# Attention scores in units of two key chunks by 512 queries instead of one chunk by 576, with the last 64 queries of a head in a unit of their own

## The chip, the cores and the metric

One core of a Trainium2 chip runs the whole program. The metric is device time in microseconds (us) from the start to the end of one execution, and the number given for the kernel before is the median of three runs. The engines are named as the profile names them: PE (TensorE matmul), PEld (its weight loads), DVE (VectorE), ACT (ScalarE), POOL (GpSimd) and SP (SyncE, which here only issues DMAs).

## The reference

Attention over 8 batches, 8 heads, 1152 keys and 576 pooled queries of width 64, followed by a mixture of experts that picks one expert of eight for each token.

```python
def _attn_ref(q, k, v):                       # q, k, v: (8, 8, 1152, 64)
    q_pool = q.reshape(B, H, S // 2, 2, D).mean(axis=3)
    scores = scale * np.matmul(q_pool, k.transpose(0, 1, 3, 2))
    scores = scores - np.max(scores, axis=-1, keepdims=True)
    attn = np.exp(scores)
    attn = attn / (np.sum(attn, axis=-1, keepdims=True) + 1e-09)
    return np.matmul(attn, v)

def _moe_ref(x, w_gate, w_output_gate, w1, w2):   # x: (4608, 512), 8 experts
    e_idx = np.argmax(x @ w_gate, axis=1)         # then for each expert e and its tokens:
    h = np.maximum(x[mask] @ w1[e], 0.0)
    out[mask] = gate_w[mask, None] * eom[mask, e, None] * (h @ w2[e])
```

## The kernel before

The attention stage works on 32 pairs of heads, four pairs to a batch. The experts' stage follows it. All numbers that need more than 16 bits are split in a high and a low float16 part, and products are summed from the parts.

For every pair there are four streams of work, and the order of the instructions on PE, DVE, ACT and POOL is the order in which the program writes them (`manual_schedule`):

- **Maxima** (`mgen`): the largest score of each query, found ahead of time. For a tile of 128 queries and a third of the keys (384) one matmul goes to one of three PSUM banks (`mp`, L320), and DVE reduces it to one column (`pm`, L321). A pair has 9 tiles of queries, so 27 such steps. They run one pair ahead. A small float32 transpose (L355), a DVE split (`mr`, L360) and a DMA bring the maxima into row 64 of `qb`, from where they enter the scores as one more term of the product.
- **Scores** (`scores`): one step is one chunk of 128 keys by all 576 queries of a head, so 18 steps for a pair. Four matmuls of 288 columns (L383 and L384, twice) fill two banks of one of two PSUM slots, `SP[0]` and `SP[1]`, taken in turn. ACT then takes the exponential twice: once as float16, `ph`, and once as float32. In odd steps (`PLP`) the float32 one stays in the slot (L402, L403), and DVE subtracts `ph` from it, bank by bank (`pl`, L407); the slot is free after that. In even steps the float32 one goes to SBUF (`p32`, L412, L413), the slot is free after the second exponential, and POOL subtracts (L414).
- **P V** (`av`): for each chunk and each of five blocks of 128 queries (the last one overlaps the fourth by 64) three matmuls of 65, 64 and 65 columns (L429 to L431), 270 for a pair, into one bank. They run `ALAG` = 6 steps behind the scores, in bursts (`BURST`) of two chunks in every other step. DVE normalises the result of a head (`norm`, L439 to L441).
- **Preparation and routing**: loads, scalings and splits of the next pairs' q, k and v (`prep`: ACT L237, L249, L277; POOL L240 to L252, L281, L284; DMAs by SP), transposes and router products of finished pairs (`logits`, L481 to L493), and after each fourth pair the routing of a batch (`router`), with five indirect DMAs on POOL (L593).

The main loop goes through 18 steps for a pair; in a step come, in this order, what waits in `pendv` (the DVE subtraction of the step before), the routers, the scores, one or two steps of maxima, and the P V burst. `tc.declare_no_dep` lets the matmuls of a slot's first bank start when DVE has finished that bank alone.

## Time and profile before

| | |
|---|---|
| median of three runs | 1332.72 us (1332.58 to 1333.58) |
| profiled execution | 1328.25 us, its span 1326.2 us |
| attention stage | ends at about 883 us of the span; the experts' stage takes the rest |
| mean granted TensorE clock | 0.992 of full speed |

The rows of the trace are in the section on rows. Starts and durations are in us from the start of the span. A matmul's duration contains the time that it takes to pass through the engine, so the time it occupies is the distance from its start to the next start; neighbouring instructions on ACT and DVE overlap at their ends as well.

### The profile page before, as it was taken

What the parts mean: (1) busy time and instruction counts of PE and PEld (TensorE: products, weight loads), DVE (VectorE), ACT (ScalarE), POOL (GpSimd) and SP (SyncE); (2) the same over time, 40 slices, a digit from 0 to 9 for tenths busy, and PEclk for the clock granted to TensorE, in tenths of its full rate; (3) what the DMA queues carried; (4) which work ended last, traced back from release to release, by engine and by line L of the source; (5) the groups of instructions that cost most, each with busy time, mean ns of one, the idle gap of its engine ahead of it and who ended that gap; (6) DMA issues with size and microseconds to landing.
All of it is one profiled execution on the core that took longest, in us unless ns stands there. A gap on an engine that the chain in (4) does not pass through costs nothing. (4 is left out here: it accounts for less than half of the span.)

```text
span 1326.2 us, 39965 instructions
## 1 busy us (share of the span) xinstructions
PE 1259.5 (95%) x15664; PEld 939.4 (71%) x15664; DVE 1088.3 (82%) x2595; ACT 1055.0 (80%) x1944; POOL 887.0 (67%) x763
## 2 busy tenths in 40 slices
PE   6999999999999999999999899998999999999997
PEld 3777777777767777777777776775667676767775
DVE  8888888888888888888888788778786767677887
ACT  6999889989989989989989788875565656566785
POOL 5888798888888889789879798756233233333431
PEclk9999999999999999999999899999999999999999
DMA  5456364445445445345535544349967676767850
GB/s 170 130 143 173 107 149 121 142 119 136 123 132 146 117 113 171 115 117 145 148 105 153 160 139 111 83 156 322 400 232 269 227 264 228 253 241 254 287 187 16
DMA packets 101272, 225.57 MB, mean 170 GB/s; under 512 B 17980, under 2 KB 33552, under 8 KB 101075
## 3 DMA queue, kind: packets, MB, share of 16 engines
q1 hardware_dynamic: 91170, 201.41, 49.9%
q0 software_dynamic: 9056, 20.85, 4.5%
q8 instruction: 125, 2.05, 0.6%
q10 hardware_dynamic: 848, 0.66, 0.2%
q14 instruction: 73, 0.59, 0.1%
HBM read 160.04 MB, written 22.50 MB: 138 GB/s over the span
## 5 line engine op out<-in xcount | busy, mean ns | idle before, releaser
L321 DVE TENSOR_REDUCE pm<-mp 128x1 f32<-128x384 f32 x864 | 449.4, 549 | 47.2 <-PE mp L320 41.6
L414 POOL TENSOR_TENSOR pl<-p,ph 128x576 f16<-128x576 f32 x291 | 375.4, 1293 | 117.3 <-ACT ph L413 98.3
L383 PE MATMUL sps<-qa,ka 128*128 128x288 f16 x1152 | 314.6, 285 | 16.2 <-DVE pl L407 9.0
L384 PE MATMUL sps<-qb,kb 65*128 65x288 f16 x1152 | 317.0, 288 | 3.3 <-DMA qb<-mr 3.3
L429 PE MATMUL av<-vt,ph 128*128 128x65 f16 x2880 | 292.9, 193 | 1.5 <-DVE xb L441 1.0
L431 PE MATMUL av<-vt,pl 128*128 128x65 f16 x2880 | 292.6, 192 | 1.4 <-POOL pl L414 1.4
L430 PE MATMUL av<-vt,ph 128*128 128x64 f16 x2880 | 293.0, 194 | 0.0
L429 PEld LDWEIGHTS <-ph 128*128 128x128 f16 x2880 | 265.9, 97 | 24.2 <-DVE xb L441 10.4
L407 DVE TENSOR_TENSOR pl<-sps,ph 128x288 f16<-128x288 f32 x558 | 228.5, 451 | 58.7 <-ACT sps L403 54.1
L430 PEld LDWEIGHTS <-ph 128*128 128x128 f16 x2880 | 264.7, 97 | 14.0 <-issue 0.3
L431 PEld LDWEIGHTS <-pl 128*128 128x128 f16 x2880 | 265.2, 99 | 1.5 <-POOL pl L414 1.5
L402 ACT ACTIVATE ph<-sps 128x576 f16<-128x576 f32 x279 | 187.2, 671 | 64.3 <-PE sps L384 55.4
L320 PE MATMUL mp<-ka,qa 128*128 128x384 f16 x768 | 215.8, 328 | 12.9 <-DVE pm L321 9.8
L965 PE MATMUL hps<-x,w1h 128*128 128x256 f16 (+2 forms) x1408 | 206.9, 260 | 1.7 <-DVE x L953 1.7
L412 ACT ACTIVATE p<-sps 128x576 f32<-128x576 f32 x291 | 193.5, 665 | 15.1 <-PE sps L384 13.7
L413 ACT ACTIVATE ph<-sps 128x576 f16<-128x576 f32 x291 | 194.0, 667 | 0.0
L403 ACT ACTIVATE sps<-sps 128x576 f32<-128x576 f32 x279 | 186.7, 669 | 0.0
L965 PE MATMUL hps<-x,w1l 128*128 128x256 f16 (+2 forms) x704 | 178.5, 260 | 0.0
L384 PEld LDWEIGHTS <-kb 65*128 65x128 f16 x1152 | 111.7, 97 | 76.1 <-issue 21.9
L979 ACT ACTIVATE hh<-hps 128x512 f16<-128x512 f32 (+2 forms) x88 | 48.2, 549 | 119.1 <-PE hps L965 116.8
L965 PEld LDWEIGHTS <-w1h 128*128 128x128 f16 x1408 | 131.7, 98 | 15.4
L383 PEld LDWEIGHTS <-ka 128*128 128x128 f16 x1152 | 117.7, 102 | 34.9 <-issue 8.7
(284 smaller groups left out, 2304.9 us busy)
## 6 DMA issues: line engine op xcount, KB each, us to landing
vp<-in_vL_dram SPq DMA_DIRECT2D x32, 576.0 KB
qp<-in_qT_dram SPq DMA_DIRECT2D x31, 576.0 KB
kpf<-in_kT_dram SPq DMA_DIRECT2D x31, 576.0 KB
ka<-xk SPq DMA_DIRECT2D x120, 144.0 KB
raw1a<-in_w_dram SPq DMA_DIRECT2D x16, 1024.0 KB
raw2a<-in_w_dram SPq DMA_DIRECT2D x16, 1024.0 KB
raw1b<-in_w_dram SPq DMA_DIRECT2D x14, 1024.0 KB
raw2b<-in_w_dram SPq DMA_DIRECT2D x14, 1024.0 KB
```

Source lines behind the costliest of these rows:

```text
L320: nc.tensor.matmul(mp, lhsT=l, rhs=r, start=j == 0, stop=j == len(ops) - 1)
L321: nc.vector.tensor_reduce(out=pm[:, i:i + 1], in_=mp, axis=AX.X, op=ALU.max)
L383: mm = [nc.tensor.matmul(sps[:, j, 0:288], lhsT=ka[:, h, ks], rhs=qa[:, o + 288 * j:o + 288 * j + 288], start=True, stop=False), nc.tensor ...
L384: nc.tensor.matmul(sps[:, j, 0:288], lhsT=kb[:, h, ks], rhs=qb[:, h, 288 * j:288 * j + 288], start=False, stop=True)]
L407: l = nc.vector.tensor_tensor(out=pl[:, 288 * j:288 * j + 288], in0=x[:, j], in1=ph2[:, j], op=ALU.subtract)
L412: nc.scalar.activation(out=p32.rearrange("p (j n) -> p j n", j=2), in_=x, func=AF.Exp, scale=1.0 / 16 / KS)
L413: e_ = nc.scalar.activation(out=ph2, in_=x, func=AF.Exp, scale=1.0 / 16 / KS)
L414: nc.gpsimd.tensor_tensor(out=pl, in0=p32, in1=ph, op=ALU.subtract)
L429: nc.tensor.matmul(av_[:, qb, 0:65], lhsT=hi, rhs=vt[:, h, c, 0:65], start=c == 0 and qb == 0, stop=False)
L430: nc.tensor.matmul(av_[:, qb, 0:64], lhsT=hi, rhs=vt[:, h, c, 66:130], start=False, stop=False)
L431: mm = nc.tensor.matmul(av_[:, qb, 0:65], lhsT=lo, rhs=vt[:, h, c, 0:65], start=False, stop=c == NC - 1 and qb == 4)
L965: d['mm'] = nc.tensor.matmul(hp[:, f, 0:w], lhsT=W1[l][g][:, c, fs], rhs=d['x'][:, c, o:o + w], start=c == 0 and i == 0, stop=c == 3 and i ...
```

## The change

A pair now has 11 units in place of 18 steps, listed in `UNITS`. Nine units 'D' are two key chunks by the first 512 queries of a head (18 chunks of the pair in order, so that the fifth one holds the last chunk of the first head and the first chunk of the second). Two units 'T' are the last 64 queries of a head with all nine chunks. The two PSUM slots are still taken in turn; since 11 is odd, a unit's slot changes from pair to pair. Units 0, 2, 4, 6, 8, 10 (`GPS`) go to POOL, the other five, all of type D, to DVE.

- Maxima: pieces of 512 keys, two for each tile; the remaining 128 keys of up to four tiles share a bank and one reduction. 21 steps for a pair in place of 27, two in a unit (one in the first T).
- P V: pieces of one chunk by four blocks, 12 matmuls; a T unit gives 27 matmuls. They run `ULAG` = 3 units behind the scores, and the pieces stand between the steps of maxima. In the units in which a head is finished (`CLOSE`) all pieces come first and the normalisation follows at once.
- Buffers: five pairs of `ph`/`pl` for D, two for T, three `p32` of 1024 columns, where there were nine, and six of 576.
- The DMA of the maxima is issued two steps later (`SLAG`), a pair's router work one step later (`DL`). The last block of 64 queries sits in partitions 0 to 63, so one of five transposes is half as large, and two copies to `xT` take the place of three.

```diff
-BURST = {0: 2, 2: 2, 4: 2, 6: 2, 8: 1, 10: 2, 12: 2, 14: 2, 16: 3}
-PLP = (1, 3, 5, 7, 9, 11, 13, 15, 17)
+UNITS = (('D', 0), ('D', 1), ('D', 2), ('D', 3), ('T', 0), ('D', 4), ('D', 5), ('D', 6), ('D', 7), ('D', 8), ('T', 1))
+PV = (((0, 2),), ((2, 4),), ((4, 6),), ((6, 8),), (0,), ((8, 9),), ((9, 12),), ((12, 14),), ((14, 16),), ((16, 18),), (1,))
+GPS = (0, 2, 4, 6, 8, 10)
+CLOSE = (5, 10)
+ULAG = 3
+SLAG = 2
+AHEAD = 21
+MX = (2, 2, 2, 2, 1, 2, 2, 2, 2, 2, 2)
-ALAG = 6
-PB = 9
-P32 = 6
+PB = 5
+PT = 2
+P32 = 3
...
-                    ch = [(t, c) for t in range(t0, t1) for c in range(3)]
+                    ch = [((t,), c) for t in range(t0, t1) for c in range(2)]
+                    ch += [(tuple(range(t, min(t + 4, t1))), 2) for t in range(t0, t1, 4)]
...
-                        nc.vector.tensor_reduce(out=pm[:, i:i + 1], in_=mp, axis=AX.X, op=ALU.max)
+                        o = pm3[:, ts[0] - t0:ts[-1] + 1 - t0, c]
+                        nc.vector.tensor_reduce(out=o, in_=mp[:, 0:w * len(ts)].rearrange("p (t k) -> p t k", t=len(ts)), axis=AX.X, op=ALU.max)
...
+            if kind == 'D':
+                ph = pp.tile([128, 2, NM], F16, name="ph", bufs=PB)
+                pl = pp.tile([128, 2, NM], F16, name="pl", bufs=PB)
+                x = sps
+                for j in range(2):
+                    g = 2 * i + j
+                    st[g] = ph[:, j], pl[:, j]
+                    product(st, sps[:, j], g // NC, g % NC, 0, NM, [] if j else seconds[u % 2])
...
+            if k in (GPSL if last else GPS):
+                p32 = p3.tile([128, 2 * NM], F32, name="p32", bufs=P32)
...
+                ex(out=p32, in_=x)
+                e_ = ex(out=ph, in_=x)
+                nc.gpsimd.tensor_tensor(out=pl, in0=p32, in1=ph, op=ALU.subtract)
...
+            else:
+                ex(out=ph, in_=x)
+                e_ = ex(out=x, in_=x)
+
+                def lo(x=x, ph=ph, pl=pl):
                     for j in range(2):
+                        l = nc.vector.tensor_tensor(out=pl[:, j], in0=x[:, j], in1=ph[:, j], op=ALU.subtract)
+                    seconds[u % 2] = [l.ins]
+                pendv.append(lo)
...
+                for i in range(max(w1 - w0, 2)):
...
+                    adv('m', mg, min(w1, w0 + i + 1))
+                    if not afirst:
+                        next(pieces, None)
```

Three places show how the order moves. The first is PE in the middle of the program, at the scores of one step on the slot `sps_133`; `ka`, `qa`, `kb`, `qb` are the parts of keys and queries, `mp` a bank of the maxima. Before:

```order
L383 LDWEIGHTS ka_139
L383 MATMUL sps_133<-qa_142,ka_139 128x288
L384 LDWEIGHTS kb_136
L384 MATMUL sps_133<-qb_145,kb_136 128x288
L383 LDWEIGHTS ka_139
L383 MATMUL sps_133<-qa_142,ka_139 128x288
L384 LDWEIGHTS kb_136
L384 MATMUL sps_133<-qb_145,kb_136 128x288
L320 LDWEIGHTS qa_140
L320 MATMUL mp_10630<-ka_137,qa_140 128x384
L320 LDWEIGHTS qa_140
L320 MATMUL mp_10633<-ka_137,qa_140 128x384
```

And PE now, at a unit on the same slot; L462 to L464 are P V of the unit three before:

```order
L389 LDWEIGHTS ka_139
L389 MATMUL sps_133<-qa_142,ka_139 128x512
L390 LDWEIGHTS kb_136
L390 MATMUL sps_133<-qb_145,kb_136 128x512
L389 LDWEIGHTS ka_139
L389 MATMUL sps_133<-qa_142,ka_139 128x512
L390 LDWEIGHTS kb_136
L390 MATMUL sps_133<-qb_145,kb_136 128x512
L332 LDWEIGHTS qd_150
L332 MATMUL mp_8033<-xk_7159,qd_150 128x128
L462 LDWEIGHTS ph
L462 MATMUL av_7864<-vt_156,ph 128x65
```

The same four matmuls are 512 columns wide, and P V begins after one step of maxima; the next step stands behind twelve matmuls of P V.

The second place is ACT, where a pair's query cast (`xq`) and value conversions (`vt`) stand between the exponentials. Before:

```order
L249 CAST xq<-qs 128x576
L402 ACTIVATE ph<-sps_133 128x576
L403 ACTIVATE sps_133<-sps_133 128x2x288
L485 COPY xT<-tp 128x256
L486 COPY xT<-tp 128x64
L412 ACTIVATE p_13727<-sps_132 128x576
L413 ACTIVATE ph<-sps_132 128x576
L277 ACTIVATE vt_154<-vp 128x9x64
L402 ACTIVATE ph<-sps_133 128x576
L403 ACTIVATE sps_133<-sps_133 128x2x288
```

The same stretch of ACT now:

```order
L443 ACTIVATE ph<-sps_132 128x1024
L444 ACTIVATE sps_132<-sps_132 128x1024
L262 CAST xq<-qs 128x576
L428 ACTIVATE p_14899<-sps_133 128x1024
L429 ACTIVATE ph<-sps_133 128x1024
L290 ACTIVATE vt_154<-vp 128x9x64
L443 ACTIVATE ph<-sps_132 128x1024
L444 ACTIVATE sps_132<-sps_132 128x1024
L290 ACTIVATE vt_154<-vp 128x9x64
L428 ACTIVATE p_15006<-sps_133 128x1024
```

The conversions now stand behind neighbouring units of 1024 columns, three of them within three units.

The third place is POOL from one pair's key split (`kp`) on, with `pl<-p` the subtraction of an even step. Before:

```order
L243 TENSOR_TENSOR kp_12152<-kpf,xk_12156 128x1152
L414 TENSOR_TENSOR pl<-p_12392,ph 128x576
L252 TENSOR_TENSOR yq<-qs,xq 128x576
L414 TENSOR_TENSOR pl<-p_12467,ph 128x576
L281 TENSOR_SCALAR vp<-vp 128x576
L414 TENSOR_TENSOR pl<-p_12536,ph 128x576
L284 TENSOR_TENSOR vt_154<-vp,vt_154 128x9x64
```

POOL now, from the same split on; `pu` is the low part of a T unit:

```order
L256 TENSOR_TENSOR kp_10619<-kpf,xk_10623 128x1152
L430 TENSOR_TENSOR pl<-p_10887,ph 128x1024
L265 TENSOR_TENSOR yq<-qs,xq 128x576
L294 TENSOR_SCALAR vp<-vp 128x576
L430 TENSOR_TENSOR pl<-p_10991,ph 128x1024
L297 TENSOR_TENSOR vt_156<-vp,vt_156 128x9x64
L294 TENSOR_SCALAR vp<-vp 128x576
L430 TENSOR_TENSOR pu<-p_11094,pt 128x576
```

There are fewer subtractions, most of them of 1024 columns, and two pieces of preparation can stand between two of them.

## Rows read from the trace of the kernel before

**Rows 1.** The page, busy time of each engine: us, share, instructions.

```profile
PE 1259.5 (95%) x15664; PEld 939.4 (71%) x15664; DVE 1088.3 (82%) x2595; ACT 1055.0 (80%) x1944; POOL 887.0 (67%) x763
```

**Rows 2.** The tile kp: POOL's split, once a pair from the second on.

```profile
L243 POOL TENSOR_TENSOR kp<-kpf,xk x31: 2364/2376/2382, 19.0 to 814.7; 128x1152 f16<-128x1152 f32 x31
```

**Rows 3.** Windows, pairs of a batch: length, PE, PEld, DVE, ACT, POOL busy; clock, DMA.

```profile
429.38:455.16 25.78, 25.37 (x391) 19.73 (x388) 22.56 (x57) 23.84 (x46) 21.32 (x17) 1.00 0.46 123
...
481.00:508.70 27.70, 25.81 (x397) 19.80 (x394) 23.96 (x67) 24.50 (x46) 24.31 (x21) 1.00 0.42 115
...
sum 105.62, PE 101.86 PEld 78.81 DVE 92.42 ACT 95.78 POOL 90.48; mean PE 25.46 PEld 19.70 DVE 23.11 ACT 23.95 POOL 22.62
```

**Rows 4.** Who waited for whom, 100 to 800 us: total, times, longest.

```profile
POOL pl L414 <- ACT ph L413: 75.7, 66, 4.8
ACT ph L402 <- PE sps L384: 47.2, 78, 2.6
DVE pl L407 <- ACT sps L403: 46.1, 140, 0.7
```

**Rows 5.** Timeline of DVE, 448 to 452 us: start, duration, wait before.

```profile
448.89 0.82 DVE L407 TENSOR_TENSOR pl<-sps,ph 128x288 f16<-128x288 f32 x2 [0.19 <-ACT sps L403]
...
451.58 0.82 DVE L407 TENSOR_TENSOR pl<-sps,ph 128x288 f16<-128x288 f32 x2 [0.19 <-ACT sps L403]
```

**Rows 6.** Timeline of PE, 449.3 to 450.2 us.

```profile
449.40 0.28 PE L383 MATMUL sps<-qa,ka 128*128 128x288 f16 x1
...
449.76 0.28 PE L383 MATMUL sps<-qa,ka 128*128 128x288 f16 x1
449.88 0.29 PE L384 MATMUL sps<-qb,kb 65*128 65x288 f16 x1
```

**Rows 7.** Timeline of ACT, 449.2 to 452 us.

```profile
450.29 0.65 ACT L402 ACTIVATE ph<-sps 128x576 f16<-128x576 f32 x1 [0.40 <-PE sps L384]
450.84 0.65 ACT L403 ACTIVATE sps<-sps 128x576 f32<-128x576 f32 x1
```

**Rows 8.** Timeline of PE: two P V matmuls, and six router products.

```profile
425.36 0.19 PE L430 MATMUL av<-vt,ph 128*128 128x64 f16 x1
425.39 0.19 PE L431 MATMUL av<-vt,pl 128*128 128x65 f16 x1
...
442.04 0.74 PE L493 MATMUL tp<-wf,xT 128*128 128x16 f32 x6
```

**Rows 9.** Timeline of PE in the experts' stage: matmuls of 512 columns.

```profile
945.57 0.38 PE L1004 MATMUL yp<-w2h,hh 128*128 128x512 f16 x1
945.79 0.38 PE L1005 MATMUL yp<-w2l,hh 128*128 128x512 f16 x1
```

**Rows 10.** Timeline of ACT in the experts' stage: 1024 columns, and what follows.

```profile
923.65 1.04 ACT L927 ACTIVATE w1h<-raw1c 128x1024 f16<-128x1024 f32 x1
924.59 0.19 ACT L927 ACTIVATION_READ_ACCUMULATOR w1h<-raw1c 128x1 f32 x1
```

**Rows 11.** Timeline of DVE in the experts' stage: two of 512 columns from PSUM.

```profile
951.71 1.28 DVE L953 TENSOR_TENSOR x<-xps,x 128x512 f16<-128x512 f32 x2
```

**Rows 12.** Groups of ACT, 100 to 800 us: busy, mean ns, idle before.

```profile
L237 ACT ACTIVATE xk<-kpf 128x576 f16<-128x576 f32 x52 | 36.1, 694 | 0.0
```

**Rows 13.** Groups of POOL, 100 to 800 us.

```profile
L414 POOL TENSOR_TENSOR pl<-p,ph 128x576 f16<-128x576 f32 x235 | 300.4, 1280 | 89.3 <-ACT ph L413 75.7 <-DVE eq L536 4.6 <-DVE es L803 1.7
...
L593 POOL DMA_INDIRECT idscr<-tid,posi x30 | 31.0, 1032 | 4.8 <-issue 3.2 <-PE mp L320 0.9 <-DMA qb<-xq 0.2
```

**Rows 14.** Timeline of PE, 734 to 736 us: the wait before a transpose.

```profile
734.62 0.27 PE L355 MATMUL tp<-ident,m 128*5 128x128 f32 x1 [1.69 <-DVE pm L321]
```

**Rows 15.** Window behind that wait; the eighth column is the granted clock.

```profile
740.00:745.00 5.00, 5.00 (x41) 3.43 (x40) 3.82 (x15) 3.07 (x6) 1.95 (x2) 0.50 0.96 385
```

**Rows 16.** Timeline of POOL, 725 to 765 us: two successive splits of kp.

```profile
727.73 2.38 POOL L243 TENSOR_TENSOR kp<-kpf,xk 128x1152 f16<-128x1152 f32 x1
...
761.86 2.37 POOL L243 TENSOR_TENSOR kp<-kpf,xk 128x1152 f16<-128x1152 f32 x1
```

More of the change, by code (lines that the diff above doesn't have):

```diff
@@ L343, in sends @@
         def sends():
-            while pendd and pendd[0][1] < now[0]:
+            while pendd and pendd[0][1] + (SLAG if now[0] > 18 else 0) < now[0]:
                 pendd.pop(0)[0]()
@@ L438, in norm, with close @@
+        def close(n, h):
+            p = pairs[n]
+            if p[0] not in xbs:
+                xbs[p[0]] = sm.tile([128, 5, XW], F32, name="xb", bufs=2)
+            xb = xbs[p[0]]
+            av_ = avt[n, h][1]
+            r = keep['rs'][:, 2 * n + h]
+            H = 2 * p[1] + h
             def norm():
@@ L602, in router @@
                 yield from setup(psum, free)
[L604 to L607 removed]
         xbs = {}
[L611 to L616 removed]
         states = {}
[L619 removed]
+        mg = mgen()
         NP = len(pairs)
@@ L690, in attention @@
+                rows()
+                if pos['m'] == NMX * NP:
+                    pop(2)
+                    for s in range(-(-t0 // 3), -(-t1 // 3)):
+                        i = PRE.get(s - 18 * (NP - 1))
+                        if i is not None:
+                            presplit(i // 2, i % 2)
+                for _ in pieces:
+                    pass
+                prep_(9)
                 if not live:
```

280 lines of the change are left out of this document (155 added, 125 removed).

## The prediction

> **What bounds the kernel now.** I read the page first: no engine is full over the span, and PE's 95% contains the time in which a matmul only passes through the pipe [rows 1], so it says little about room. The change touches the attention stage alone, so I went to that stage and to its unit of repetition, the pair. POOL's key split marks it: 30 intervals from 19.0 to 814.7 us are 26.5 us each [rows 2]. Windows cut at those marks show a batch of four pairs in 105.6 us: 25.8 for a plain pair, 27.7 for the longest one [rows 3]. ACT is busy 95.8 of the 105.6, DVE 92.4, POOL 90.5: three engines near nine tenths, none at ten. Such a picture means a ring of waits, and the list of waits shows it: POOL waits for ACT, ACT for PE, DVE for ACT [rows 4].
>
> The ring is that of the slot that DVE empties. From one DVE subtraction to the next on that slot 2.69 us pass, for two steps [rows 5]. Inside: the second bank is free 0.82 after the start (448.89 to 449.71); PE starts on it 0.05 later, at 449.76, its last matmul at 449.88 ends at 450.17 [rows 6]; ACT begins 0.12 later, after 0.40 of idling, and its second exponential ends at 451.49 [rows 7]; DVE begins 0.09 later. In stretches in which ACT has conversions as well, ACT itself sets the pace.
>
> What each engine would need if it never waited, for a pair: PE 72 score matmuls at 0.12 [rows 6], 270 of P V at 0.03 [rows 8], 27 maxima at 0.16 (384/512 of the 0.22 between two matmuls of 512 columns [rows 9]), 17 small float32 products and transposes at 0.1 to 0.12 (the last of six starts about 0.5 after the first [rows 8]), 8.7 + 8.1 + 4.4 + 1.9 = 23.1 us. ACT 36 exponentials at 0.55 [rows 7], five conversions at about 0.58 (694 ns less an overlap of 0.1 at the end [rows 12]), copies 0.6: 23.3. So a plain pair of 25.8 loses 2.5 us of its two fullest engines' time.
>
> **The change part by part.**
>
> *PE's work* hardly changes. The score columns are the same, 20736 for each of the two products; 36 matmuls of 512 at 0.216 and 40 of 64 or less, which I price like P V's at 0.03 (same weights, same width), are 9.0 against 8.7. P V stays at 270. Maxima keep their columns: 4.4. PE still needs 23.3.
>
> *ACT.* An exponential of 1024 columns appears nowhere in the attention stage. The nearest row is a copy with scale of 1024 columns, followed 0.94 later [rows 10]; by columns from the 576 it would be 0.98. I take 0.94, since there the length is the same. 18 x 0.94 + 4 x 0.55 = 19.1 against 19.8. With the conversions 22.5.
>
> *DVE.* Two subtractions of 512 take 1.28 together, the second starting 0.60 after the first [rows 11]. For the same columns less the start of eight instructions about 0.6 us are saved; six reductions fewer save some 0.4. At nothing: DVE is busy 92.4 of 105.6 and ACT's exponentials cover it. Were that cover gone, the pair would gain this 1 us.
>
> *POOL.* A subtraction of 576 takes 1.28, the split of 1152 takes 2.38 [rows 2, 13], so 1024 take about 2.1. Four of these and two of 1.28 against nine: 11.0 against 11.5. Nothing, as POOL waits for ACT.
>
> *The new ring*, in the same steps as above: the second bank is free 1.28 after the start, 0.05, one matmul interval 0.22 and one duration 0.38 [rows 9], 0.12, 0.94 + 1.04, 0.09: 4.1 us for two D units. They carry 2048 columns where 2.69 carried 1152; per column 2.0 ns against 2.3. That is the gain: the fixed links of the ring are paid 4.5 times in a pair and not nine times.
>
> *A plain pair walked through.* PE needs in a D unit 0.86 (scores) + 0.72 (24 P V) + 0.43 (two maxima) = 2.0, in a T unit 0.60 + 0.72 + 0.22 = 1.5; ACT 1.9 and 1.1. The rules: PE starts a unit's scores when it is through with the unit before and the slot is free (0.74 after a DVE subtraction's start for the first bank, 1.33 for the second; 2.05 after ACT's start on a POOL unit); ACT starts 0.72 after PE's start on the second bank, or when it is through with the unit before and what stands between. Counted from ACT's start on unit 0, ACT starts unit 1 at 2.0 (PE's scores were last), 2 at 4.0 (PE), 3 at 6.5 (ACT: one key conversion of 0.58), T0 at 9.2 (ACT: another, and a copy), 5 at 10.6 (ACT: a copy), 6 at 13.1 (ACT: the query cast), 7 at 15.7 (PE: 1.1 of router products in two units), 8 at 18.2 (ACT: two value conversions), 9 at 20.1 (ACT), T1 at 22.1 (PE). DVE subtracts unit 9 from 20.1 + 2.07 = 22.2 on, PE starts on the second bank at 23.5, and ACT on the next unit 0 at 24.2; it idles 1.1 there, since T1 was short. So 24.2 us for a plain pair. The same account of the pair before (four rings of 2.69, five stretches bound by ACT with 2.2 and 3.5 of extras) gives 25.1 and the trace says 25.8; 0.7 a pair escapes such an account. The pair after is 24.2 to 24.9; I take 24.6, near the middle.
>
> *Longer pairs.* A batch takes 105.6 - 4 x 25.8 = 2.4 more than four plain pairs. Routing brings five indirect DMAs of 1.03 to POOL [rows 13]; they are not removed, so I leave the 2.4.
>
> *At nothing*: the maxima's later DMA (a pair of lead covers it; without that, ACT would stand before it), half a transpose, two copies for three (0.1 in a pair), the buffers (P V frees a D pair of buffers about two units before it is needed again), SP's queue (the same DMAs at the same place in a pair). P V waits for POOL in no plain pair of this walk: unit 8's subtraction is the tightest; ACT is done with unit 8 at 20.2, POOL 2.1 later, at 22.4, and PE comes to its P V at 24.0, behind the next unit 0's scores and one step of maxima. The two ends of the stage, filling and draining, keep their lengths within a microsecond or two: three units behind are 6.6 us, six steps were 8.6.
>
> *One long pair.* Between the splits at 727.73 and 761.86 lie 34.1 us [rows 16], 7.7 above the mean. In it PE waited 1.69 for DVE [rows 14], and a few microseconds later the granted clock was 0.50, the lower level of 1.2 GHz [rows 15]. It is where the experts' setup joins routing. It may return or not; I count half, 3.9.
>
> *Sum*: 8 batches x 4 x (25.8 - 24.6) = 38, and 4: 42 us. From the profiled execution's own 1328 us (span 1326.2 and 2 around it) that gives 1286; the median of the runs stands 4.5 above that execution, so I say **1290 us**. At 24.2 and with the long pair gone: 51 + 8, 1274. At 24.9: 29 and nothing, 1304.
>
> **Rivals.**
>
> *The gain is half eaten by P V (1304 to 1328, about 1314).* P V of a unit follows after three units, and its low part now comes from one subtraction of 2.1 in place of 1.28. In a pair with five indirect DMAs (5.2 in all, most of them ahead of T1 in POOL's queue) T1's low part would be ready at 29, while PE wants it at 27.9. If PE waits 0.1 at each of the six POOL units, that is 0.6 a pair and 19 us. For it: POOL has little room in routing pairs, 24.3 busy of 27.7 [rows 3]. Against it: the margins of 1.6 and more above. The Trainium skill (Perfetto Trace Analysis, Optimizing Scalar/DVE Operations) says that where such engines are not saturated but cause gaps on others, instructions should be broken up, which speaks against this change. The trace agrees in that ACT and DVE idle while they hold up others [rows 4]; but the ring per column gets shorter with the larger pieces, so I give the rule this rival's chance.
>
> *Slower: PE's clock (1336 to 1356).* The place is a batch's routing pair, where T1's low part is late by one or two microseconds. One wait of 1.69 was followed by a stretch at half clock, and the pair lost 7.7 [rows 14 to 16]. If each of eight batches did this, 62 us would be lost against the 38 gained: 1290 + 4 + 62 = 1356. It decides from six such pairs on (38/7.7 = 5, and one was there before). Against it: over the whole span the mean granted clock is 0.992, in spite of all of PE's shorter waits. The Trainium skill (TensorE: Matmul & The Clock Gate, HAM oscillation) describes this kind of repeated fall between bursts of matmuls; the trace shows one.
>
> *No change (1330 to 1335).* PE's 23.3 is untouched, and a loss of 2.5 a pair could simply come back at other places, such as the T units, in which ACT has 1.1 of work and PE 1.5. For that all twelve waits would have to move; the walk finds three.
>
> *More (below 1274).* The 0.7 that escapes my account belongs to the number of steps, 18 against 11; then the pair is 24.2 or less and routing shrinks as well: 1262 to 1274.
>
> **How the numbers follow.** My case (1274 to 1304) 0.55, half eaten 0.18, slower 0.14, no change 0.05, more 0.08. Faster by over 0.2% (about 2.7 us, what a measurement here can tell from no change): 0.55 + 0.18 + 0.08 = 0.81; same 0.05; slower 0.14. The range of 8 in 10 leaves out the slower case and a little at the other end: 1266 to 1328.
>
> **What would show it.** Right: splits of kp about 25.2 us apart on average; two exponentials of 1024 columns 0.94 apart; two subtractions on DVE in 1.28; a ring of 4.1 to 4.3 us between subtractions on one slot; ACT idle mainly at the start of a pair. Wrong: P V waiting for POOL's `pl` or `pu` (half eaten), windows with a granted clock near 0.5 (slower), exponentials of 1.2 or more, or matmuls of 64 columns well above 0.03.

## The result: 14 us faster, a third of the gain that was forecast

The changed kernel took 1319.3 us (1317.05 to 1322.65) against 1333.15 us (1332.58 to 1338.22) for the kernel before, a ratio of 0.989 (0.986 to 0.992). Two more comparisons of the same two kernels on other chips gave 0.987 (0.984 to 0.990) and 0.988 (0.986 to 0.991). Chips differ by up to 0.8% for one and the same kernel (medians of before: 1323 to 1334), so runs of different comparisons are set against each other by these ratios, never by their times; differences of ratios of some 0.3% between two chips are not read as effects (run 14 shows why). The forecast was 1290, so 42 us; 14 to 19 came.

The page, busy time of each engine, as in [rows 1], of the changed kernel:

```profile
PE 1250.5 (95%) x15792; PEld 867.7 (66%) x15792; DVE 1053.9 (80%) x2154; ACT 1022.0 (77%) x1463; POOL 862.7 (65%) x665
```

Every engine has less to do, ACT by 33 us and DVE by 34. The windows of one batch, as in [rows 3] but cut at DVE's normalisation of a pair's first head (L506), which marks a pair here (length, busy PE, PEld, DVE, ACT, POOL, clock, DMA share, GB/s):

```profile
454.00:481.40 27.40, 25.99 (x400) 17.91 (x399) 23.74 (x61) 23.12 (x32) 22.07 (x15) 1.00 0.57 159
481.40:508.20 26.80, 25.00 (x392) 17.41 (x390) 21.33 (x43) 23.04 (x30) 24.88 (x19) 1.00 0.44 120
508.20:532.90 24.70, 24.59 (x392) 17.33 (x390) 21.19 (x42) 22.72 (x30) 20.87 (x14) 1.00 0.45 128
532.90:557.90 25.00, 24.35 (x390) 17.14 (x389) 21.29 (x44) 23.03 (x30) 21.16 (x16) 1.00 0.45 127
sum 103.90, PE 99.93 PEld 69.79 DVE 87.55 ACT 91.92 POOL 88.98; mean PE 24.98 PEld 17.45 DVE 21.89 ACT 22.98 POOL 22.25
```

The two plain pairs take 24.8 and 24.9 by exact marks, near the forecast's 24.6. But two pairs of the batch are longer: the one in which the batch is routed (26.9 to 27.4 in most batches), and the one behind it (26.8). POOL issues the five indirect DMAs of the routing between 471 and 490 us, the first two before the mark at 481.4 and three behind it. By the same marks a batch of the kernel before was 28.5, 25.8, 25.8 and 25.6, so it had one longer pair. The batch went from 105.7 to about 103.4, not to 100.8.

Waits from 100 to 800 us, as in [rows 4] (engine and line, what for, total, times, longest):

```profile
POOL pl L430 <- ACT ph L429: 72.0, 60, 3.7
DVE pm L334 <- PE mp L332: 62.3, 85, 2.1
ACT p L428 <- PE sps L390: 34.1, 68, 2.7
DVE pl L448 <- ACT sps L444: 30.8, 70, 0.5
...
ACT sl L621 <- DVE sl L620: 11.6, 7, 1.7
...
PE av L464 <- POOL pu L430: 6.0, 6, 1.2
...
PE sps L390 <- DMA qb<-mr: 4.6, 5, 1.7
```

The first four are those of the main stream. ACT's two waits for scores (this one and 17.7 at L443) come to 51.8 where they were 58.2, DVE's for ACT to 30.8 from 46.1, but DVE's wait for the maxima's matmuls is 62.3 where it was 33.3. The other three are what the study had to weigh: ACT behind DVE in the router, PE behind POOL for the low part of the last unit, PE behind the maxima's DMA.

### The profile page after: what moved, and what is told of

Read it like the earlier page. It is cut to its first block, busy times and chain, and to the rows that moved or that the text cites. A ratio compares the mean times of both kernels' runs of the same rounds, so it can differ in the third digit from the quotient of the medians.

```text
span 1320.6 us, 38792 instructions
## 1 busy us (share of the span) xinstructions
PE 1250.5 (95%) x15792; PEld 867.7 (66%) x15792; DVE 1053.9 (80%) x2154; ACT 1022.0 (77%) x1463; POOL 862.7 (65%) x665
## 4 chain that ended last, share of the span: by engine, by line
PE 68%; DVE 13%; ACT 7%; POOL 4%; issue 4%; DMA 3%; DVEq 0%; POOLq 0%; ACTq 0%
PE hps L1050 15%; PE sps L389 7%; PE mp L332 7%; PE sps L390 6%; PE yp L1089 5%; PE yp L1090 5%; PE av L462 5%; PE yp L1092 5%; PE av L464 4%; PE av L463 4%; DVE pm L334 3%; PE tp L555 3%; DVE pl L448 2%; ACT ph L443 2%; ACT sps L444 2%
## 5 line engine op out<-in xcount | busy, mean ns | idle before, releaser
L334 DVE TENSOR_REDUCE pm<-mp 128x1 f32<-128x512 f32 (+2 forms) x672 | 423.1, 664 | 76.1 <-PE mp L332 71.6
L430 POOL TENSOR_TENSOR pl<-p,ph 128x1024 f16<-128x1024 f32 x128 | 272.6, 2132 | 108.8 <-ACT ph L429 88.6
L390 PE MATMUL sps<-qb,kb 65*128 65x512 f16 (+2 forms) x1216 | 268.2, 281 | 4.6 <-DMA qb<-mr 4.6
L462 PE MATMUL av<-vt,ph 128*128 128x65 f16 x2304 | 264.2, 193 | 5.1 <-DVE xb L506 3.8
L389 PE MATMUL sps<-qa,ka 128*128 128x512 f16 (+2 forms) x1216 | 267.3, 281 | 1.4 <-DVE pl L448 1.4
L464 PE MATMUL av<-vt,pl 128*128 128x65 f16 x2304 | 262.9, 193 | 3.6 <-POOL pl L430 3.2
L462 PEld LDWEIGHTS <-ph 128*128 128x128 f16 x2304 | 216.3, 97 | 57.3 <-DVE xb L506 21.6
L463 PEld LDWEIGHTS <-ph 128*128 128x128 f16 x2304 | 214.0, 97 | 45.7 <-issue 2.3
L448 DVE TENSOR_TENSOR pl<-sps,ph 128x512 f16<-128x512 f32 x310 | 199.3, 685 | 39.6 <-ACT sps L444 37.8
L332 PE MATMUL mp<-ka,qa 128*128 128x512 f16 (+1 forms) x768 | 209.7, 327 | 13.4 <-DVE pm L334 6.5
L464 PEld LDWEIGHTS <-pl 128*128 128x128 f16 x2304 | 214.6, 99 | 4.4 <-POOL pl L430 4.1
L428 ACT ACTIVATE p<-sps 128x1024 f32<-128x1024 f32 (+1 forms) x192 | 173.3, 903 | 50.8 <-PE sps L390 43.1
L443 ACT ACTIVATE ph<-sps 128x1024 f16<-128x1024 f32 x155 | 158.9, 1025 | 34.4 <-PE sps L390 22.7
L444 ACT ACTIVATE sps<-sps 128x1024 f32<-128x1024 f32 x155 | 158.8, 1025 | 0.0
L429 ACT ACTIVATE ph<-sps 128x1024 f16<-128x1024 f32 x128 | 130.5, 1020 | 0.0
L390 PEld LDWEIGHTS <-kb 65*128 65x128 f16 x1216 | 97.5, 98 | 46.8 <-issue 4.7
```

What stands on the lines that cost most here:

```text
L332: nc.tensor.matmul(mp[:, w * j:w * j + w], lhsT=l, rhs=r, start=True, stop=True)
L334: nc.vector.tensor_reduce(out=o, in_=mp[:, 0:w * len(ts)].rearrange("p (t k) -> p t k", t=len(ts)), axis=AX.X, op=ALU.max)
L389: for m in (nc.tensor.matmul(out, lhsT=st['ka'][:, h, ks], rhs=st['qa'][:, o + q0:o + q1], start=True, stop=False), nc.tensor.matmul(out, ...
L390: nc.tensor.matmul(out, lhsT=st['kb'][:, h, ks], rhs=st['qb'][:, h, q0:q1], start=False, stop=True)):
L430: nc.gpsimd.tensor_tensor(out=pl, in0=p32, in1=ph, op=ALU.subtract)
L443: ex(out=ph, in_=x)
```

## The experiments

Each kernel is the changed kernel with the edit shown, unless another base is named. "Batch" is the time of four pairs by the marks above; a stretch with the experts' setup or a fall of the clock is named where it is included.

**1. The router's exponentials later.** Two steps between DVE's results and ACT's small exponentials.

```diff
+            if b < nb - 1:
+                yield
+                yield
             late.append(nc.scalar.activation(out=ex[:, :, 0:8], ...
```

(and the same ahead of the exponential of `sl`).

> The changed kernel, with the router's two small exponentials issued one unit later on ACT than the DVE instructions that feed them (all batches but the last). Theory A (in a routing pair ACT stands in order behind DVE: 1.7 us at sl and 1.0 us at exg, 2.7 us a batch): the first of a batch's two longer pairs, 26.9 us, comes down to 25.2 to 25.9, 1.0 to 1.7 us over eight batches, and the kernel to 1306 to 1312 us against 1319.3. Theory B (POOL's load in routing pairs sets the extra): the two waits go and the time stays within 2 us of 1319, since ACT is held up later by something else. A third way: DVE's sum sx now waits for ACT, and the time rises by some us.

Ratio 0.986 (0.984 to 0.988). Both waits of ACT are gone, and a batch still takes 103.5 to 103.8 where it had 103.3 to 104.3 with the changed kernel on an undisturbed stretch: the longer pairs became 28.3 and 25.6. Theory A, my first explanation, falls: the waits of ACT that this edit takes away did not set the time of the batch.

**2. The indirect DMAs spread.**

```diff
-                for _ in range(3):
+                for _ in range(7 if b < nb - 1 else 3):
                     yield
                 i = nc.gpsimd.indirect_dma_start(
```

> The changed kernel, with the five indirect DMAs of a batch's routing seven half units apart on POOL, not three (all batches but the last), so that a pair has three of them and not five. Theory B (in the pair of the five DMAs POOL, 1.03 us each, is late with the low part of the last unit, and PE waits 1.1 us for it): the second longer pair of a batch, 26.9 us, comes down to 25.3 or so, 1.2 to 1.6 us over eight batches, 1307 to 1310 us. Theory A alone: no change, 1317 to 1321 us, since what is late there was late already.

Ratio 0.985 (0.983 to 0.987), batches 101.6 to 103.5. In some of them the second longer pair is gone (24.8), in others it is 26.2 to 26.6. PE no longer waits for `pu`; it now waits 10.3 us, in eight places, for the maxima's DMA. POOL was part of the loss, and a new wait took much of it back. The edit also delays the experts' setup, by some 20 us (its copy L899 begins at 721.8 and not at 701.2 as in run 5), so the ratio holds more than the DMAs; the batches ahead of the setup do not.

**3. P V four units behind.**

```diff
-ULAG = 3
+ULAG = 4
-PB = 5
+PB = 6
```

> The changed kernel, with P V four units behind the scores and not three, and a buffer pair more. If PE's waits for POOL's low parts (8.7 us in the stage) are lost on the path: 1309 to 1313 us, and no wait of PE on pl or pu is left. If they only take the place of other waits of PE: 1317 to 1321 us. The drain of the stage gets one unit longer, about 2 us, so 1321 to 1323 is what it costs if nothing is won.

Ratio 1.021 (1.016 to 1.025): slower by some 44 us than the changed kernel (1.021 against 0.988), which none of the theories had. No wait of PE for `pl` or `pu` is among the larger ones any more, but a plain pair takes 26.1 to 26.3. DVE now stands 28.3 us (38 times) in front of the normalisation, behind PE's last P V, where the changed kernel has 5.2 us (6 times): the lag also decides beside which unit a head is closed, and what stands behind the normalisation in DVE's queue waits with it. But PE also waits 20.0 us (17 times) for the maxima's DMA, in the changed kernel 4.6, and 13.9 us (24 times) for DVE's `pl`. Which of the three makes the 44 us is not shown, and the run does not tell what the waits for POOL alone cost.

**4. The maxima alone.** The kernel before with the new pieces of 512 keys and 21 steps a pair.

```diff
-                    ch = [(t, c) for t in range(t0, t1) for c in range(3)]
+                    ch = [((t,), c) for t in range(t0, t1) for c in range(2)]
+                    ch += [(tuple(range(t, min(t + 4, t1))), 2) for t in range(t0, t1, 4)]
```

> The kernel before, with only the maxima changed: 21 steps a pair, 512 keys by one reduction and the last 128 of up to four tiles by one, in place of 27 of 384 keys. The prediction costed this part at nothing: 1331 to 1335 us. Rival: DVE's 0.4 us (six reductions fewer) to 1 us a pair is felt, as DVE is 92.4 of 105.6 us busy: 1301 to 1320 us, and then the score units brought less than the whole change. A second rival: the reduction of 512 keeps DVE longer at a time and holds up the subtraction behind it: 1336 to 1345 us.

Ratio 1.002 (1.001 to 1.004), plain pairs 26.0 where they were 25.7: alone, in the kernel before, the maxima gain nothing and cost some 3 us. So the reductions saved on DVE are no gain there; whether they are one beside the wide units no run shows.

**5. The changed kernel on the next three's chip.**

> The changed kernel once more, on the chip on which the next three run, so that they can be set against it: by the ratio 0.989 (0.986 to 0.992) about 11 to 18 us below the kernel before on that chip. If the clock's three falls (560, 710 and 850 us) belong to the order of the work, they stand at the same places; if they are chance, at others.

Ratio 0.987 (0.984 to 0.990). The profiled execution was the fastest of four (1306 to 1316): the falls of the clock at 565 and 850 us are absent, the one behind the setup (705 to 710, clock 0.50) is there.

**6. Unit 3 by POOL in routing pairs.**

```diff
-            if k in (GPSL if last else GPS):
+            if k in (GPSL if last else GPS + (3,) if n and n % 4 == 0 else GPS):
```

> The changed kernel, with the low part of unit 3 made by POOL and not by DVE in the pairs in which a batch is routed (seven of 32). Theory C (in the first half of a routing pair DVE is the bound: 12.2 us busy of 13.3, with the router's some twenty small instructions in one dense chain with its subtractions and maxima; 1.28 us go to POOL, which is busy 8.7 of 13.3): the pair of 27.4 us comes down by 0.8 to 1.3, over seven batches 6 to 9 us, so 0.5 to 0.7% under the changed kernel. Theory A (ACT standing behind DVE): the waits at sl and exg get shorter by some tenths, 1 to 3 us in all. If POOL is the bound there too: no change.

Ratio 0.985 (0.982 to 0.988), every batch but the one with the setup 103.3 to 103.5. The unit was the wrong one: the router's instructions stand around unit 9, six units on. What it shows is that 1.28 us moved from DVE to POOL in a plain stretch are worth nothing.

**7. The experts' setup later.**

```diff
+                for _ in range(22):
+                    yield
                 yield from setup(psum, free)
```

> The changed kernel, with the experts' setup 22 half units later, so that it falls into a plain pair and not on the heels of a batch's routing. If the long pair (38.0 us, 13 above a plain one, with the granted clock at 0.84 after PE had waited 3.3 us) is the setup on top of routing: the pair comes to 27 or less and its neighbour to 27, 6 to 9 us less in all, and no granted clock under 0.95 there. If the setup's own chain of small DVE instructions is enough: the long pair moves with it and the time stays within 3 us.

Ratio 0.982 (0.978 to 0.987) against 0.987 for run 5 beside it. The long pair and its neighbours went from 34.0, 29.1, 24.9 to 26.8, 27.5, 30.5, without a fall of the clock. Against pairs of the same kind without it (26.8, 24.8, 24.9, 26.9) the setup costs some 9 us wherever it lies, and some 12 on top of the routing. That is less than half of the 6 to 9 us that were expected, and the two ratios' intervals overlap.

**8. The maxima's DMAs two steps earlier.**

```diff
-SLAG = 2
+SLAG = 0
```

> The changed kernel, with the maxima's DMAs issued two steps earlier, as the kernel before had them. The prediction costed this edit at nothing since a pair of lead would cover it; PE waited 4.6 us in five places for that DMA, and a fall of the clock followed one of them (1.4 us at 563.8). If the edit cost something: no wait of PE on that DMA is left and the time is 2 to 6 us lower. If not, within 2 us; and if ACT then stands before the DMA's semaphore in each pair (0.1 to 0.3 us, 64 times), 6 to 19 us higher.

Ratio 0.986 (0.981 to 0.990); the waits for that DMA are gone, the batches are the same. Alone it is worth nothing that can be measured.

**9. Unit 9 by POOL in routing pairs** (the edit of run 6 with `(9,)`).

> The changed kernel, with the low part of unit 9 made by POOL and not by DVE in the pairs in which a batch's routing begins (seven of 32). Unit 9 is the one whose subtraction stands between the router's instructions (456.9 us in the run before this one); unit 3 stood in a plain stretch. Theory C (there DVE is one dense chain and sets the pace): the half pair of 12.8 us comes to 11.7 to 12.0, over seven batches 6 to 8 us, about 0.5% under the changed kernel. Theory A' (PE and ACT stand behind the router's own instructions, whatever DVE has to do besides): less than 0.4 a batch, no change that can be measured. POOL has units 8, 9, 10 and 0 in a row then; if it becomes late, PE waits for its low parts of unit 9 and the pair gets longer by up to 1 us.

Ratio 0.989 (0.984 to 0.993), no change. PE's waits for the maxima's DMA were 11.5 us (12 times), and one batch took 107.7 with a fall of the clock.

**10. Spread DMAs and early maxima's DMAs** (the edits of runs 2 and 8).

> The changed kernel, with the indirect DMAs seven half units apart and the maxima's DMAs two steps earlier. Apart, the first took a batch from 103.4 to 101.6 to 103.5 and left PE 10.3 us of waits for the maxima's DMA in place of POOL's; the second did nothing. If the two waits hide one another: every batch 101.6 or less (two us less than the changed kernel, 14 in all), no wait of PE on that DMA, and the time 1.0 to 1.2% under the changed kernel. If the DMA is late for another reason than its issue: batches as with the first edit alone, 0.3 to 0.6%.

Ratio 0.970 (0.966 to 0.974), 1.9% under the changed kernel and more than its two parts together. The same windows of a batch:

```profile
448.50:475.30 26.80, 25.73 (x400) 17.88 (x399) 23.67 (x60) 22.90 (x32) 21.94 (x15) 1.00 0.46 129
475.30:500.10 24.80, 24.69 (x392) 17.40 (x391) 21.23 (x43) 22.85 (x30) 22.71 (x16) 1.00 0.58 164
500.10:525.00 24.90, 24.78 (x392) 17.28 (x390) 21.31 (x42) 22.87 (x30) 23.11 (x17) 1.00 0.47 129
525.00:549.90 24.90, 24.25 (x389) 17.09 (x388) 21.23 (x42) 22.95 (x30) 21.13 (x16) 1.00 0.45 127
```

The second longer pair is a plain one. In the five batches between the first one and the setup a batch takes 103.7 in run 5, 103.6 with the maxima's DMAs earlier (run 8), 102.6 with the indirect DMAs spread (run 2) and 101.7 with both: together they are worth more than one by one, by some 0.8 a batch. The ratio has more than that. Between the profiles of run 5 and this one lie 15.0 us at the last mark: 10.0 in these five batches, 6.6 in the two with the setup, less 1.6 ahead of them; run 5's profile is the fastest of its four executions. The setup too is later here, and its copy took 0.48 us and not 3.18 (run 17).

What the maxima's DMA had to do with it, in run 2, in three views. First DVE and ACT's queue (making `mr`, sending it):

```profile
381.77 0.27 DVE L373 TENSOR_SCALAR mr<-tp 4x128 f16<-4x128 f32 x1
...
384.49 0.62 ACTq L148 DMA_DIRECT2D qb<-mr  x1
```

Then PE (start, duration, wait before), and the window ahead of it:

```profile
392.12 0.38 PE L390 MATMUL sps<-qb,kb 65*128 65x512 f16 x1 [1.27 <-DMA qb<-mr]
```

```profile
390.00:392.00 2.00, 0.85 (x4) 0.31 (x4) 0.67 (x2) 0.94 (x3) 1.91 (x2) 1.00 0.92 194
```

The DMA was sent 2.7 us after DVE began to make its data. PE wanted it 6.4 us after the sending and could go on 1.27 later, 7.6 after it, while the next pair's loads and key copies kept the DMA engines busy from 386 us on (share 0.86, 1.19, 0.92 in three windows of 2 us); that they delayed it is likely, but not tested. In run 10 it was sent 0.55 us after that start, and PE waits for it nowhere. Alone the earlier sending brought nothing (run 8): as long as POOL made the pair longer, this wait had time. Once POOL was out of the way, it was next.

**11. Run 10 with the setup later** (runs 2, 7 and 8).

> Both edits of the run before, and the experts' setup 22 half units later. If the long pair's loss is the setup on top of a batch's routing: 3 to 9 us less than the run before; batches 101.6 and the batch with the setup 106 to 110; 1.5 to 1.8% under the changed kernel, 2.7 to 3.1% under the kernel before. If the spread DMAs and the setup now meet: as the run before.

Ratio 0.969 (0.964 to 0.974), as run 10. The spread DMAs delay the setup already; 22 half units more bring it to the next batch's routing (28.0 and 31.0).

**12. Run 11 with unit 9 by POOL.**

> The three edits of the run before, and unit 9's low part by POOL in the routing pairs. Theory C: batches of 100.5, 5 to 8 us less than the run before. Without it: as the run before, within 3 us. POOL late: 2 to 6 us more.

Ratio 0.971 (0.967 to 0.975). The batches are 100.7 to 101.1, and the routing pair is 26.2 for 26.9: theory C holds for 0.7 of the 2.1 us, once the other waits are gone. The long pairs (28.0 and 36.5, with the clock at 0.65 from 760 and at 0.50 from 780 us) took back more than that.

**13. The changed kernel on the chip of the next three.**

> The changed kernel once more, on the chip of the next three, as what they are set against: 0.987 to 0.989 of the kernel before.

Ratio 0.988 (0.986 to 0.991).

**14. Run 10 with unit 9 by POOL.**

> The indirect DMAs seven half units apart, the maxima's DMAs two steps earlier, and unit 9's low part by POOL in the routing pairs, with the setup where the changed kernel has it. Theory: the first two give 101.5 a batch (0.9696 of the kernel before), the third 0.7 a batch more, as the run with four edits showed (26.2 for 26.9 in the routing pair): 0.966 to 0.969 of the kernel before, 20 to 28 us under the changed kernel. Rival: the third is lost in the long pair, as it was with four edits: 0.970.

Ratio 0.973 (0.971 to 0.975), 21 us under run 13 on the same chip; batches 100.6 to 101.8. The routing pair in the windows:

```profile
445.90:472.10 26.20, 25.63 (x400) 17.83 (x399) 22.52 (x59) 23.09 (x32) 24.04 (x17) 1.00 0.47 132
```

DVE has 22.5 us in it and not 23.7, POOL 24.0 and not 21.9; the pair is 0.7 shorter by exact marks. Seven times 0.7 is 5 us, or 0.35%; the ratio does not show it, and is even higher than run 10's on another chip (0.973 against 0.970, with intervals that overlap).

**15. Run 14 with the setup at half its pace.**

```diff
             V.tensor_copy(out=ms, in_=mx)
             V.tensor_tensor(out=eq, in0=cn, in1=ms.broadcast_to([128, 8]), op=ALU.is_equal)
-            yield
+            yield 1
```

(and at the setup's five other steps).

> The run before, with the experts' setup at half its pace (a step for each unit, not two). If the long pairs (28 to 36 us with the setup, at a granted clock of 0.5 to 0.9 behind waits of PE for DVE) come from DVE's chain of small setup instructions between its subtractions: 25 to 27 us there and no fall of the clock, 4 to 8 us less than the run before. If they come from the chip's clock alone or from the indirect loads that end the setup: the same time within 3 us.

Ratio 0.971 (0.969 to 0.972), 1.5 us under run 14, with intervals that overlap. The pairs with the setup are 27.3 and 26.1, as expected, but the next, a routing pair, took 31.0, at a granted clock of 1.00 throughout. The trace shows what stands there: the four indirect loads that end the setup, one behind the other on POOL, then the subtraction for which ACT and PE wait.

```profile
754.04 1.09 POOL L851 DMA_INDIRECT xg<-xrows,ids  x1 [0.27 <-PE mp L332]
...
758.05 1.00 POOL L851 DMA_INDIRECT xg<-xrows,ids  x1 [0.30 <-issue]
...
759.33 2.13 POOL L430 TENSOR_TENSOR pl<-p,ph 128x1024 f16<-128x1024 f32 x1
```

```profile
761.50 1.02 ACT L428 ACTIVATE p<-sps 128x1024 f32<-128x1024 f32 x1 [3.36 <-POOL pl L430]
761.52 0.20 PE L464 MATMUL av<-vt,pl 128*128 128x65 f16 x1 [2.35 <-POOL pl L430]
```

So part of the setup's cost lies in these loads, as the second theory has it; DVE's chain costs something too, since the pairs with it became shorter. No run takes the loads apart. The profiled execution was the slowest of five, by 4 us.

**16. The last unit's low part by DVE.** The DMAs stay together; unit 10 leaves POOL in the pairs that have them (with run 8's edit).

```diff
-            if k in (GPSL if last else GPS):
+            if k in (GPSL if last else GPS[:-1] if n > 4 and n % 4 == 1 else GPS):
```

> The changed kernel with the maxima's DMAs two steps earlier, and the low part of the last unit (T1) made by DVE, not by POOL, in the pairs with the five indirect DMAs, which stay three half units apart. Theory B (POOL is late with that low part, since five DMAs of 1.03 us stand ahead of it): the second longer pair goes from 26.9 to 24.8 to 25.3 without any change to the DMAs, a batch to 101.4 to 102, and the kernel to 0.970 to 0.975 of the kernel before. Rival B' (the DMAs themselves hold something else, the SP queue or the maxima's DMAs): the pair stays at 26.5 or more and the time at 0.985 to 0.989.

Ratio 0.986 (0.984 to 0.988). The second longer pair fell from 26.8 to between 25.6 and 25.7 in four of six batches (26.2 and 26.5 in the other two) and no wait for `pu` is left among the larger ones; run 13 has 6.9 us of them. Theory B is borne out for 1.2 of the pair's 2.0 us, which is what PE had waited for `pu` (1.15); what holds the other 0.8, which goes when the DMAs are spread, is not shown. The time did not follow, and is the one that the rival had named: this execution has falls of the clock at 695, 735 and 840 us, to 0.5 to 0.6, and all five have a mean clock of 0.985 to 0.991.

**17. One copy in the setup in another form.**

```diff
-                V.tensor_copy(out=k['oh1'], in_=oh)
+                V.tensor_tensor(out=k['oh1'], in0=em, in1=mi.broadcast_to([128, 8]), op=ALU.is_equal)
```

> The changed kernel, with one instruction of the experts' setup in another form: DVE's copy of 128x8 values from one SBUF tile to another (L899), which took 2.6 to 3.2 us in five of the runs with the pieces of POOL back to back beside it and 0.3 to 0.6 in others, becomes the comparison that made those values (one operand in PSUM, 0.15 us in the same trace). The Trainium skill (SBUF: State Buffer, Who contends with whom) says that such a copy and an instruction of GpSimd exclude one another. If that hold makes the long pair: PE's wait of 3.3 us for DVE is gone, the pair of 34 to 35 us comes to 27 to 29, no fall of the clock there, and the kernel 4 to 9 us under the changed one: 0.981 to 0.985 of the kernel before against 0.988. If the setup's other instructions make it: the instruction takes 0.15 us and the pair stays above 32, the time within 3 us.

Ratio 0.981 (0.979 to 0.983), clear of the changed kernel's three intervals, which are from other chips. The timelines of the changed kernel show what is held, DVE, POOL and PE:

```profile
705.12 3.19 DVE L899 COPY oh<-ohe 128x8 f32<-128x8 f32 x1
```

```profile
702.71 4.22 POOL L430 TENSOR_TENSOR pl<-p,ph 128x1024 f16<-128x1024 f32 x2
706.88 1.40 POOL L259 TENSOR_TENSOR qs<-qp 128x576 f32<-128x576 f32 x1
708.36 1.15 POOL L253 TENSOR_SCALAR kpf<-kpf 128x1152 f32<-128x1152 f32 x1
```

```profile
709.23 0.44 PE L547 MATMUL tp<-ident,xb 128*128 128x128 f32 x2 [3.27 <-DVE pm L334]
```

A copy of eight columns begins at 705.12 and ends at 708.31, in the gap after POOL's three instructions. In the new form it took 0.16 us and PE's wait of 3.3 us is gone. Windows of run 13 (the copy took 3.18 us), then of run 17:

```profile
700.00:705.00 5.00, 3.70 (x56) 2.30 (x55) 4.18 (x12) 3.74 (x5) 5.00 (x4) 1.00 0.33 118
705.00:710.00 5.00, 2.67 (x38) 2.33 (x39) 4.90 (x11) 1.30 (x3) 2.53 (x3) 0.67 0.88 252
710.00:715.00 5.00, 5.00 (x55) 3.20 (x53) 1.67 (x7) 2.28 (x4) 3.60 (x2) 0.65 0.30 79
```

```profile
700.00:705.00 5.00, 4.13 (x70) 2.77 (x67) 4.17 (x16) 3.74 (x6) 5.00 (x4) 1.00 0.32 118
705.00:710.00 5.00, 5.00 (x80) 3.61 (x77) 3.83 (x12) 3.95 (x7) 4.84 (x4) 1.00 0.97 280
710.00:715.00 5.00, 3.77 (x41) 2.41 (x39) 3.03 (x14) 3.15 (x5) 3.80 (x3) 0.86 0.53 136
```

The fall of the clock from 705 on is not there; a shallower one (0.86, then 0.80) comes with the next wait of PE, 1.2 us for the key copies at 711.9, and the pair is 32.5 for 34.2. So the copy is one cause of the long pair, and the setup's other instructions remain one. Its share is small: 1.7 us in that pair, and by the profiles the last mark stands at 853.6, where it was 852.9 and 855.5 in runs 5 and 13. Most of the ratio's 0.7% is not found in the trace. The five executions have mean clocks of 0.995 to 0.996, the changed kernel's from 0.988 to 0.996, so that fewer falls may be the rest; that is argued.

**18. Run 15 with that copy changed**: all five edits together, and the lowest ratio.

> The best version so far (DMAs spread, maxima's DMAs earlier, unit 9's low part by POOL in routing pairs, setup at half pace; 0.9705 of the kernel before) with the same instruction changed. There the copy took 1.2 us. If the hold matters: 1 to 3 us less, 0.968 to 0.970. If not: 0.9695 to 0.9725.

Ratio 0.966 (0.963 to 0.968): 1286.8 against 1334.2 us for the kernel before on that chip, and 2.3% under the changed kernel by the ratios; 0.968 to 0.970 was expected. The step from run 15 (0.971 on another chip) is not much larger than what ratios differ by between chips, so it is not shown to be the copy's.

## Why the prediction was wrong

The time came out in the band of the first rival (1304 to 1328), which had 0.18, but not by its main term: in a plain pair PE waits for none of POOL's low parts.

**Right: the prices, and the order of the walk.** From one exponential of 1024 columns to the next 0.92 pass (priced 0.94), POOL's subtraction of 1024 took 2.13 (priced 2.1), DVE's pair of 512 1.29 (priced 1.28). DVE's subtractions in a plain pair of the changed kernel, as in [rows 5]:

```profile
413.42 1.29 DVE L448 TENSOR_TENSOR pl<-sps,ph 128x512 f16<-128x512 f32 x2 [0.53 <-ACT sps L444]
...
417.91 1.29 DVE L448 TENSOR_TENSOR pl<-sps,ph 128x512 f16<-128x512 f32 x2
...
422.26 1.29 DVE L448 TENSOR_TENSOR pl<-sps,ph 128x512 f16<-128x512 f32 x2 [0.52 <-ACT sps L444]
...
427.28 1.29 DVE L448 TENSOR_TENSOR pl<-sps,ph 128x512 f16<-128x512 f32 x2 [0.31 <-ACT sps L444]
...
431.88 1.28 DVE L448 TENSOR_TENSOR pl<-sps,ph 128x512 f16<-128x512 f32 x2
```

These are units 1, 3, 5, 7 and 9. They are 4.49, 4.35, 5.02 and 4.60 apart, and 6.31 to the next unit 1; the walk's starts of ACT have 4.5, 4.1, 5.1, 4.4 and 6.1.

**Failed: "That is the gain: the fixed links of the ring".** No ring of 4.1 to 4.3 us for two D units is there. The 4.35 contain the short T0, so 1600 columns; where two D units follow one another, it is 4.49 to 5.02, and ACT has a conversion in each. ACT in the same pair, answering [rows 7]:

```profile
409.32 1.02 ACT L428 ACTIVATE p<-sps 128x1024 f32<-128x1024 f32 x1 [0.87 <-PE sps L390]
...
418.54 0.68 ACT L428 ACTIVATE p<-sps 128x576 f32<-128x576 f32 x1
...
420.29 1.02 ACT L443 ACTIVATE ph<-sps 128x1024 f16<-128x1024 f32 x1 [0.21 <-PE sps L390]
421.21 1.02 ACT L444 ACTIVATE sps<-sps 128x1024 f32<-128x1024 f32 x1
...
432.03 0.65 ACT L428 ACTIVATE p<-sps 128x576 f32<-128x576 f32 x1 [0.53 <-PE sps L390]
```

The waits of 0.40 in [rows 7] are gone from the D units, and 1.6 us have come in their place around the two T units. In the plain pairs ACT idled 1.94 us before and idles 1.98 now (medians of five batches). So the 0.9 that a plain pair gained is as much as the work that ACT no longer has: busy 22.79 and 22.95 us, from 23.84 and 23.70. The forecast had 0.8 from that work and 0.4 from shorter waits. That the loss could come back at the T units stands in the rival "no change", at 0.05. This is read from the traces; no run has the wide units without the rest.

**Mis-sized by it: the plain pair.** 24.8 to 24.9 for 25.7 by the marks, so 0.9 a pair and not 1.2; over 32 pairs 29 us and not 38.

**Failed: "Longer pairs ... I leave the 2.4".** In the kernel before, the pair behind the routing pair, with four of the five indirect DMAs, was a plain one (25.8). In the changed kernel it is 2.0 above one. POOL in that pair, with the wait of PE that ends the head:

```profile
482.71 1.05 POOL L655 DMA_INDIRECT idscr<-tid,posi  x1 [0.27 <-issue]
483.79 2.15 POOL L430 TENSOR_TENSOR pl<-p,ph 128x1024 f16<-128x1024 f32 x1
...
489.33 1.04 POOL L655 DMA_INDIRECT idscr<-tid,posi  x1 [0.28 <-PE mp L332]
490.39 1.29 POOL L430 TENSOR_TENSOR pu<-p,pt 128x576 f16<-128x576 f32 x1
```

```profile
491.74 0.20 PE L464 MATMUL av<-vt,pu 128*128 128x65 f16 x1 [1.15 <-POOL pu L430]
```

Five DMAs of 1.05 us stand among pieces of up to 2.4 us, T1's low part is late, and PE waits 1.15 us. The prediction had this number, 29 against 27.9, in its first rival, and gave it 0.18 since the plain pairs had margin; the margin of the plain pairs said nothing of that pair. Seven times 2.0 us is 14 us. The routing pair gave some of it back: it was 2.7 above a plain pair and is 2.0 above one, so a batch's longer pairs cost 4.0 and not 2.7. Of the 4.8 us forecast for a batch 2.3 came: 1.2 are missing in the plain pairs' pace and 1.3 here. Runs 10 and 16 show the cause: spread the DMAs (with the maxima's DMAs earlier), or take T1's low part from POOL, and the pair is 24.8 or 25.6.

**Failed: "At nothing: the maxima's later DMA (a pair of lead covers it)".** There is no pair of lead: in the changed kernel PE waited for this DMA in five places, and wanted it there 3.5 to 6.7 us after it was sent, in the kernel before 7.6 us after. Alone it cost little (run 8), but it stood right behind the first fault and kept part of its removal from paying (run 2 against run 10). With both edits the ratio is 0.970, some 39 us below the kernel before. That this is near the forecast's 42 is partly luck: the plain pair still has 0.9 and not 1.2, and the setup's stretch and the filling of the stage bring what it lacks.

**Failed: half of the long pair.** Forecast 3.9 us of gain. It came to 34 to 35 us by the marks, from 31.7: the setup's copy is held behind POOL's longer runs (3.2 us against 0.7 in the kernel before), and the clock falls behind it. The rule for such a copy is in the Trainium skill (SBUF — State Buffer, Who interferes with whom): a plain copy on DVE, if it runs in a mode that takes the port pair shared with GpSimd, and an instruction of GpSimd block one another in full. The trace agrees, with 3.19 us for what takes 0.16 us in a form with one operand in PSUM (run 17); here the copy was held beyond the one instruction that ran when it began, through the whole next one. Run 17 gives the copy 1.7 us of the pair; the rest is the setup's other work.

**The clock.** The slower rival, a fall in each routing pair, did not happen; in the first profile of the changed kernel three stretches of the attention stage fell (0.66 at 565 to 570, 0.66 to 0.69 around 710 to 725, 0.50 at 850), each after PE had waited 1.4 to 3.3 us; waits of 1.70 and 1.47 us at 733 and 742 us were followed by none. Their number varies from one execution to the next (run 5 had one), and the executions of the changed kernel spread over some 6 to 10 us, the slower ones with the lower mean clock (in run 5, 1306 us at 0.995 and 1316 at 0.990). The first profile is 13.6 us ahead of the kernel before at the last mark, run 5's 22.4; the pairs with the falls are most of the difference.

**Also missed: the filling.** The prediction put the ends of the stage within a microsecond or two. The first mark stands at 42.1 to 42.4 us in the three profiles of the changed kernel and at 46.8 before, 4.4 to 4.7 earlier, and the time behind the last mark is no longer for it (451 us, in two of the three). Part of the measured gain is this, and not the units' pace.

**Open.** What makes the remaining 1.4 us of the routing pair, and how the setup's cost divides between DVE's small instructions and POOL's four indirect loads (run 15). From the last mark to the end the first profile took 458.8 us, 8 more than the kernel before; but the runs of the five later comparisons took 451 to 452, 451 to 455, 458 to 460, 451 to 452 and 451, so this may go with the chip rather than with the change; the kernel before was profiled only once.

## What to carry to other kernels

When pieces become larger, walk the pairs that have extra work, not the plain one: an engine with a tenth of its time free in the mean has none where five other instructions stand in its queue. A step priced "at nothing because it has lead" deserves a measured lead: the time from its issue to its first use, in the stretch where the transfers are thickest. Compare the idle time of the engine that sets the pace, before and after: here it did not change, and the gain was only the work saved. And when removing one wait brings less than it should, look for the wait directly behind it and remove both before giving up the theory.

## What was not expected of the hardware

- A DVE copy of 128x8 float32 values between two SBUF tiles took 2.6 to 3.2 us in six executions (the first profile, runs 5, 6, 8, 9 and 13). Each time it ended in the first gap of 0.1 us between POOL's instructions, not with the one that ran when it began. In the others it took 0.3 to 2.0; in run 16 (2.0 us) and the kernel before (0.73) it ended in such a gap too. The comparison that replaced it took 0.16.
- One wait of PE of 1.4 to 2 us in a stretch that was not full was, in some executions, followed by a stretch at the lower of the clock's two levels, 1.2 GHz and not 2.4 (means of 0.5 to 0.85 in windows of 5 us), and the pair lost 3 to 6 us: more than the wait itself. The same wait does not always do it: the last pair has one of 1.53 us, for DVE, in ten of these profiles. A fall followed in the first one and in runs 1, 9 and 16 (the pair took 27.6 to 29.4), none in runs 5, 6, 7, 8, 13 and 17 (23.8).
